# Whole DFT tables and DMA transposes in a fused Fourier and feed-forward kernel

## The chip, the cores and the metric

The kernel runs on one core of one Trainium2 chip. The metric is the device time of one execution, in microseconds; the kernel before takes 851.64 us (median of 3 runs, 851.37 to 852.25).

Names in what follows: PE is TensorE, which does the matmuls (PEld: its weight loads), ACT is ScalarE, DVE is VectorE, POOL is GpSimd; SP is the sync engine, whose queue issues most of the transfers (SPq in the traces). An evacuation is the copy of a matmul's result from PSUM to SBUF, by ACT or DVE.

## The reference

Two layers, one after the other, over 8 batches of 3008 tokens with 256 channels:

```python
X = rfft(x, axis=1)                       # x: (8, 3008, 256)
Yr = Xr @ w_r - Xi @ w_i + b_r
Yi = Xr @ w_i + Xi @ w_r + b_i
Yr, Yi = soft_threshold(Yr, 0.01), soft_threshold(Yi, 0.01)
y = irfft(Yr + 1j * Yi, n=3008, axis=1)   # (24064, 256) tokens for the next layer
h = y @ w_in                              # 256 -> 2048
g = s * maximum(h, 0) ** 2 + b
out = g @ w_out                           # 2048 -> 256, float32
```

The kernel writes 3008 as 94 x 32 and does each transform in two steps as matmuls with tables. The additive b leaves as a bias: b times the sum of w_out over its 2048 rows.

## The kernel before

Batch 0 is transformed first. From then on the feed-forward layer runs in 48 tiles of up to 512 tokens, 16 slots each (a slot is about 1.05 us), and the transform of the next batches is woven into the slots by a plan: the first step (`s1_units`), the second step with mixing and inverse (`s23_units`) and the last step (`s4_units`). The parts that the change and the argument touch:

```python
# x of a batch: four loads of 376 KB with a cast, issued from GpSimd; 4 buffers in all,
# so the loads for batch b+1 wait until the first step of batch b has read its own
def emit_load_x(b, first=None):
    for c in range(N2 // XCH):
        t = xpool.tile([P, XCH * D], F16, name="x16", tag="x16")
        if first is not None:
            gate = nc.gpsimd.tensor_copy(out=t[0:1, 0:1], in_=first)
        ...  # nc.gpsimd.dma_start(out=t[0:N1, ...], in_=xv[...])

# first step: tokens come out on the wrong axis; DRAM turns them
def s1_units(b, more_banks=False):
    ud = dpool.tile([96, N2, D], F16, name="ud", tag="ud")       # DRAM
    def unit(i):                                                 # 16 units a batch
        nc.tensor.matmul(ps[0:96, :], A_t[0:N1, :],              # 512 columns
                         x16[(b, c)][0:N1, j * D : (j + 2) * D], ...)
        evac(u[0:96, j : j + 2, :], ps[0:96, :], 512)
        ...  # u -> ud by DMA, and after the last unit ud -> us, four DMAs

# feed-forward: relu on ACT, square mostly on DVE
nc.scalar.activation(out=rt, in_=ps, func=AF.Relu)
nc.vector.tensor_tensor(out=gt, in0=rt, in1=rt, op=ALU.mult)

# sum of w_out for the bias, on GpSimd, during batch 0
def sum_w_out():
    nc.gpsimd.tensor_tensor(out=acc, in0=w_out_t[:, 0:2], in1=w_out_t[:, 2:4], op=ALU.add)
    for q in range(4, MC, 2):
        nc.gpsimd.tensor_tensor(out=acc, in0=acc, in1=w_out_t[:, q : q + 2], op=ALU.add)
    nc.gpsimd.tensor_tensor(out=w_sum, in0=acc[:, 0], in1=acc[:, 1], op=ALU.add)

# the plan for batches 2 to 7; s0, s1, s2 are the first slots of batches b-2, b-1, b
schedule(s0 + 40, s1 - s0 - 48, s1_units(b))     # first step: spread over most of a batch
schedule(s1 + 2, s2 - s1 - 30, s23_units(b))
schedule(s2 - 14, 12, s4_units(b))
if b + 1 < B:
    plan.setdefault(s1 + 6, []).append(lambda b=b: emit_load_x(b + 1))
```

In batch 0, the block-shaped tables F_t, F_2 and T_t are put together by ACT and DVE from compact ones, and each half of the result e is turned by 32 matmuls with the identity and four evacuations.

## Time and profile before

| | before |
|---|---|
| median of 3 runs (range) | 851.64 us (851.37 to 852.25) |
| profiled run: span, granted TensorE clock | 849.4 us, 0.997 |
| feed-forward tiles 0, 2, 6 and 47 (of 0 to 47) begin at | 49.6, 77.3, 149.3, 823.8 us |

TensorE (PE) is the bound after 58 us. First, when the loads of x are issued. This is the order of time on GpSimd (start us, duration us, engine, line, operation, count, and in brackets the idle time before it and what ended that):

```profile
113.50 0.52 POOL L189 DMA_DIRECT2D x<-in_x_dram  x1 [14.25 <-PE psf L562]
125.97 0.52 POOL L189 DMA_DIRECT2D x<-in_x_dram  x1 [11.95 <-PE psf L562]
138.50 0.52 POOL L189 DMA_DIRECT2D x<-in_x_dram  x1 [12.01 <-PE psf L562]
```

Each load is released by the first step (L562) of the batch before it, and because that step is spread out, so are the loads: one every 12.5 us. In the table of DMA issues (count, size, median us from issue to landing) they land fast:

```profile
x<-in_x_dram POOLq DMA_DIRECT2D x28, 376.0 KB, 5.9
```

Second, GpSimd's sums and DVE's squares, from the order of time on each. The six equal sums take 7.31 us, some 1.2 each, before the squares of the feed-forward tiles set in; those run at 10.31/9 = 1.15 us each:

```profile
40.84 7.31 POOL L331 TENSOR_TENSOR acc<-acc,w_out_t 128x512 f32<-128x512 f32 x6
```

```profile
54.91 10.31 DVE L775 TENSOR_TENSOR gt<-rt 128x1024 f16<-128x1024 f32 x9
```

A stretch of the steady state to compare with (stretch, length, busy us and counts of PE, PEld, DVE, ACT, POOL, then granted clock, DMA share, GB/s). PE is full:

```profile
150.00:158.00 8.00, 8.00 (x67) 6.29 (x66) 5.91 (x9) 5.92 (x9) 0.00 (x0) 1.00 0.47 138
158.00:166.00 8.00, 8.00 (x64) 6.33 (x63) 7.30 (x13) 5.47 (x8) 0.00 (x0) 1.00 0.18 49
```

### The profile page before, as it was taken

The page shows a single profiled execution, that of the slowest core. Times are in us where ns is not written, and L with a number is a line of the kernel's source. Part 1 is how long each engine was busy: PE and PEld are TensorE (multiplying, and loading weights), DVE is VectorE, ACT ScalarE, POOL GpSimd, SP SyncE. Part 2 cuts the span into 40 slices and gives each one's busy share as a digit, 9 for nine tenths or more (in the row PEclk, how much of TensorE's full clock was granted, in tenths as well). Part 3 has the DMA queues.
Part 4 walks back from the last instruction along what each step waited for, and adds up shares of the span by engine and source line. Part 5 has one row for each costly group of instructions (what it writes and reads, how often), then busy time and mean ns, then how long its engine had stood idle before and what let it go on. Part 6 is the DMA issues. An engine that isn't in the chain of part 4 may idle for free.

```text
span 849.4 us, 17085 instructions
## 1 busy us (share of the span) xinstructions
PE 835.0 (98%) x6645; PEld 600.5 (71%) x6645; DVE 697.0 (82%) x1027; ACT 643.2 (76%) x856; POOL 46.6 (5%) x72
## 2 busy tenths in 40 slices
PE   8899999999999999999999999999999999999997
PEld 7757777777677766777677776777667777766765
DVE  6898987888888987888878888888977888776674
ACT  5898887787778787787777887787877787766673
POOL 5321000000000000000000000000000000000000
PEclk9999999999999999999999999999999999999999
DMA  7937457324761367324662247613354223411111
GB/s 165 161 104 162 108 148 185 101 76 100 177 186 54 92 159 184 109 78 103 171 177 65 74 106 199 172 40 92 100 156 118 62 79 98 112 33 38 38 44 50
DMA packets 105458, 95.07 MB, mean 112 GB/s; under 512 B 9510, under 2 KB 97578, under 8 KB 104034
## 3 DMA queue, kind: packets, MB, share of 16 engines
q1 hardware_dynamic: 98930, 79.57, 32.6%
q0 software_dynamic: 6448, 14.42, 10.7%
q8 instruction: 52, 0.85, 0.4%
q14 instruction: 28, 0.23, 0.1%
HBM read 52.54 MB, written 46.66 MB: 117 GB/s over the span
## 4 chain that ended last, share of the span: by engine, by line
PE 88%; DVE 4%; ACT 3%; DMA 2%; issue 1%; POOL 0%; SPq 0%; DVEq 0%; ACTq 0%; POOLq 0%
PE psa L832 36%; PE psh L761 36%; PE psf L627 4%; PE psf L562 2%; PE psf L613 2%; PE psf L598 2%; PE psf L657 2%; PE psf L710 2%; ACT rt L768 1%; DVE gt L775 1%; DMA x<-in_x_dram 1%; DMA out_dram<-ost 1%; PE psh L410 1%; ACT yt L160 0%; ACT vs L160 0%
## 5 line engine op out<-in xcount | busy, mean ns | idle before, releaser
L768 ACT ACTIVATE rt<-psh 128x1024 f32<-128x1024 f32 (+2 forms) x384 | 387.1, 1009 | 119.1 <-PE psh L761 117.7
L775 DVE TENSOR_TENSOR gt<-rt 128x1024 f16<-128x1024 f32 (+2 forms) x321 | 384.0, 1199 | 98.1 <-ACT rt L768 97.4
L832 PE MATMUL psa<-w_out_t,gt 128*128 128x256 f16 (+1 forms) x3024 | 454.3, 272 | 0.1
L832 PEld LDWEIGHTS <-gt 128*128 128x128 f16 (+1 forms) x3024 | 300.9, 101 | 187.2 <-issue 1.7
L761 PE MATMUL psh<-yt,w_in 128*128 128x512 f16 (+1 forms) x1344 | 396.7, 378 | 0.3 <-ACT rt L768 0.3
L761 PEld LDWEIGHTS <-w_in 128*128 128x128 f16 x1536 | 142.9, 98 | 27.4 <-issue 2.1
L842 DVE SCALAR_TENSOR_TENSOR ost<-psa,s_bc,bias_bc 128x512 f32<-128x512 f32 (+2 forms) x97 | 71.0, 732 | 8.3 <-PE psa L832 7.1
L772 ACT ACTIVATE gt<-rt 128x1024 f16<-128x1024 f32 (+2 forms) x63 | 66.2, 1050 | 1.0
L632 DVE TENSOR_TENSOR ring<-psf,s 128x512 f16<-128x512 f32 x84 | 57.5, 684 | 3.7 <-PE psf L627 2.9
L160 ACT CAST v<-psf 128x512 f16<-128x512 f32 x78 | 45.3, 582 | 18.7 <-PE psf L657 18.7
L160 ACT CAST xf<-psf 128x512 f16<-128x512 f32 x82 | 47.9, 585 | 10.9 <-PE psf L598 10.8
L160 ACT CAST u<-psf 96x512 f16<-96x512 f32 x77 | 44.5, 580 | 11.0 <-PE psf L562 10.7
L761 PE MATMUL psh<-tail,w_in 128*128 128x512 f16 (+1 forms) x192 | 52.1, 353 | 0.0
L627 PE MATMUL psf<-W_g,xf 128*128 128x256 f16 x336 | 50.4, 273 | 0.0
L160 ACT CAST yt<-psf 128x480 f16<-128x480 f32 (+2 forms) x75 | 38.1, 520 | 13.6 <-PE psf L710 13.6
L189 POOL DMA_DIRECT2D x<-in_x_dram x36 | 18.9, 530 | 429.3 <-PE psf L562 428.0
L562 PE MATMUL psf<-x,A_t 94*96 94x512 f16 x104 | 39.7, 381 | 1.7 <-ACT yt L160 0.5
L638 DVE TENSOR_TENSOR ring<-ring,high 128x512 f16<-128x512 f16 x84 | 35.5, 423 | 2.3
L639 DVE TENSOR_TENSOR ring<-ring 128x512 f16<-128x512 f16 x84 | 35.5, 422 | 1.9
L637 DVE TENSOR_TENSOR ring<-ring,low 128x512 f16<-128x512 f16 x84 | 35.4, 421 | 1.6
L627 PEld LDWEIGHTS <-xf 128*128 128x128 f16 x336 | 32.9, 98 | 3.8
L710 PE MATMUL psf<-C_t,vs 96*128 96x96 f16 x448 | 33.0, 205 | 0.1
(89 smaller groups left out, 501.9 us busy)
## 6 DMA issues: line engine op xcount, KB each, us to landing
out_dram<-ost SPq DMA_DIRECT2D x152, 128.0 KB
ud<-u SPq DMA_DIRECT2D x28, 384.0 KB
us<-ud SPq DMA_DIRECT2D x28, 384.0 KB
vd<-v SPq DMA_DIRECT2D x42, 256.0 KB
vs<-vd SPq DMA_DIRECT2D x14, 768.0 KB
x<-in_x_dram POOLq DMA_DIRECT2D x28, 376.0 KB, 5.9
ring<-ring SPq DMA_DIRECT2D x280, 32.0 KB
out_dram<-ost SPq DMA_DIRECT2D x16, 120.0 KB
```

What stands on the lines that cost most here:

```text
L160: return None, nc.scalar.copy(out=dst, in_=src)
L562: nc.tensor.matmul(ps[0:96, :], A_t[0:N1, :], x16[(b, c)][0:N1, j * D : (j + 2) * D], start=True, stop=True,)
L627: nc.tensor.matmul(ps[:, r, :], xt[:, 2 - r, dc], W_g[:, dc, r], start=(dc == 0), stop=(dc == DC - 1),)
L632: nc.vector.tensor_tensor(out=t, in0=ps, in1=hold[i // 2][:, i % 2].unsqueeze(1).to_broadcast([P, 2, D]), op=ALU.add,)
L638: nc.vector.tensor_tensor(out=m, in0=m, in1=high, op=ALU.min)
L710: nc.tensor.matmul(ps[:, j * 96 : (j + 1) * 96], vs[(b, h)][:, k, ec * P : (ec + 1) * P], C_t, start=True, stop=True,)
L761: nc.tensor.matmul(o, w_in_t[dc][:, mc * P : (mc + 1) * P], r, start=(dc == 0), stop=(dc == DC - 1),)
L768: nc.scalar.activation(out=rt[:, :, 0:w], in_=ps[:, :, 0:w], func=AF.Relu)
L772: nc.scalar.activation(out=gt[:, :, 0:w], in_=rt[:, :, 0:w], func=AF.Square)
L775: nc.vector.tensor_tensor(out=gt[:, :, 0:w], in0=rt[:, :, 0:w], in1=rt[:, :, 0:w], op=ALU.mult)
L832: nc.tensor.matmul(ps[0:size, h, :], gts[(ti, mc // 2)][:, mc % 2, sub * size : (sub + 1) * size], w_out_t[:, mc, :], start=(mc == 0), sto ...
L842: nc.vector.scalar_tensor_tensor(out=ost[0:size, 0:k], in0=ps[0:size, 0:k], scalar=s_bc[0:size], in1=bias_bc[0:size, 0:k], op0=ALU.mult, o ...
```

## The change

Its intent: less work for PE in the first step of batches 2 to 7 (the data as the weight, 96 columns a matmul), with the turn done by two DMA transposes a batch from SBUF instead of a trip through DRAM; and in batch 0 fewer copies on ACT and DVE (the tables are loaded whole) and one half of e turned by one DMA transpose. Since that transpose stands ahead of the load of w_out, the sums of w_out come later, and the bias is made later. The diff, cut to its core (cuts marked, pool and buffer sizes left out):

```diff
     def emit_load_inverse():
-        nc.sync.dma_start(out=F_c[:, H:]..., in_=F_d[:, H:])
-        t_load = nc.sync.dma_start(out=T_c, in_=T_d)
+        nc.sync.dma_start(out=T_t[:, 0:H], in_=t_d[:, 0:H])        # whole tables
+        nc.sync.dma_start(out=F_t[:, H:], in_=f_d)
+        nc.sync.dma_start(out=F_2[1], in_=f_2_d)
+        t_load = nc.sync.dma_start(out=T_t[:, H:], in_=t_d[:, H:])
 ...
-        nc.gpsimd.dma_start(out=w_out_t, in_=moe_w_out...)         # beside w_in
 ...
-            k = i - U - 2
-            if 0 <= k < 4:
-                turn(0, k)
-            if 0 <= k - 1 < 4:
-                last_dft(0, 8 * (k - 1))
+            if i == U + 1:
+                nc.sync.dma_start(out=vs[0][:, :, 0:P],            # turn_by_dma(0)
+                                  in_=vt[0]..., transpose=True)
+                gate = nc.gpsimd.tensor_copy(out=w_out_t[0:1, 0, 0:1], in_=vs[0][0:1, 0, 0:1])
+                with tc.issue_after(gate.ins):
+                    nc.gpsimd.dma_start(out=w_out_t, in_=moe_w_out...)
 ...
+        def unit_late(i):                                          # first step, b = 2..7
+            for j in range(4):
+                nc.tensor.matmul(
+                    ps[:, j * 96 : j * 96 + 96], x16[(b, c)][0:N1, lo : lo + P],
+                    A_t[0:N1, :], start=True, stop=True,
+                )
+            evac(u[:, dc, :, 4 * g : 4 * g + 4], ps[:, 0:384]..., 384)
+            if g == N2 // 4 - 1:                                   # twice a batch
+                nc.sync.dma_start(
+                    out=us[b][:, :, dc * P : (dc + 1) * P],
+                    in_=u[:, dc].rearrange("p k n -> p (k n)"), transpose=True,
+                )
 ...
-    plan.setdefault(15, []).append(make_bias)
+    plan.setdefault(22, []).append(make_bias)
 ...
-        schedule(s0 + 40, p - 48, s1_units(b))
+        schedule(s1 - 36, 22, s1_units(b))
```

## The prediction

> **What bounds the kernel now.** I read the busy times of each engine first, then the stretches (busy time by window), then the order of time on PE, to get the pace of each shape of matmul, and last the first 58 us on ACT and DVE.
>
> The busy times put PE at 98%, but its ends are modelled, so that alone proves little.
>
> ```profile
> PE 835.0 (98%) x6645; PEld 600.5 (71%) x6645; DVE 697.0 (82%) x1027; ACT 643.2 (76%) x856; POOL 46.6 (5%) x72
> ```
>
> The stretches (busy us of PE, PEld, DVE, ACT, POOL, then granted clock, DMA share, GB/s) cut the run in two:
>
> ```profile
> 0.00:14.60 14.60, 11.60 (x144) 10.73 (x144) 7.71 (x17) 6.08 (x12) 8.13 (x16) 0.88 0.81 165
> 14.60:58.00 43.40, 38.09 (x416) 28.50 (x417) 38.42 (x61) 37.16 (x57) 18.76 (x22) 1.00 0.65 131
> 58.00:150.00 92.00, 91.52 (x717) 65.33 (x715) 80.36 (x125) 73.94 (x103) 4.90 (x12) 1.00 0.63 155
> 150.00:300.00 150.00, 149.87 (x1181) 111.00 (x1180) 128.25 (x204) 117.73 (x160) 3.18 (x5) 1.00 0.42 110
> 450.00:600.00 150.00, 149.95 (x1173) 107.53 (x1172) 128.99 (x202) 117.33 (x158) 3.00 (x5) 1.00 0.39 103
> ```
>
> After 58 us PE is never free. Between 14.6 and 58 us (batch 0's transform and the first tile) PE, DVE and ACT are each busy for 37 to 38.5 of 43.4 us: there the evacuations of PSUM are as much the limit as PE is. Before 14.6 us the load of x sets the pace.
>
> The order of time on PE (start, us, x how many) gives the pace, as the distance from a row to the next one:
>
> ```profile
> 143.61 0.38 PE L710 MATMUL psf<-C_t,vs 96*128 96x96 f16 x5
> 143.82 0.57 PE L761 MATMUL psh<-yt,w_in 128*128 128x480 f16 x2
> ...
> 233.03 0.60 PE L832 MATMUL psa<-w_out_t,gt 128*128 128x256 f16 x4
> 233.47 0.38 PE L562 MATMUL psf<-x,A_t 94*96 94x512 f16 x1
> 233.69 0.60 PE L761 MATMUL psh<-yt,w_in 128*128 128x512 f16 x2
> 234.12 0.60 PE L832 MATMUL psa<-w_out_t,gt 128*128 128x256 f16 x4
> ```
>
> 96 columns take 0.21/5 = 0.042 us, 256 take 0.44/4 = 0.11, the first step's 512 columns 0.22, the other 512 0.43/2 = 0.215. From all start-to-start distances of the trace I took off columns/2.4 + 2.5 ns for each matmul: 15.2 us are left over before 60 us, and only 5.6 us in the other 789 us. So after 60 us the time is the sum of PE's paces, and only what changes that sum counts there.
>
> **What the Trainium skill says.** "TensorE: Matmul & The Clock Gate", Back-to-back issue gap, has N/2.4 + 2.5 ns when warm; the trace agrees at 96, 128, 256 and 512 columns (42, 56, 109, 216 ns medians). The same section gives about 81 ns for a sustained stream of weight load and matmul at N = 128; here that stream runs at 56, so I use the trace. For the DMA transpose, "DMA: Bandwidth & Descriptors", Latency and other measured facts, gives 261 GB/s, 350 to 400 if contiguous; "VectorE: DVE Perf Modes", The three transpose paths, gives 1309 ns for one 128x128 by the DMA crossbar. One transpose here is 24 such blocks (0.79 MB) or 32 (1.05 MB): by the first page an estimate of 3 to 4 us, by the second, if blocks go one by one, 31 and 42 us. The trace of the kernel before holds no DMA transpose and can't decide. "DMA: Bandwidth & Descriptors", Issuing engines are not separate DMA queues, says that all queues share the same 16 engines; the trace agrees: from 20 to 38 us the casting loads of x and the weights alone fill them (DMA share about 1).
>
> **Part 1: the first step of batches 2 to 7.** Removed: 16 matmuls of 512 columns a batch, 16 x 0.22 = 3.52 us of PE. Added: 64 of 96 columns with x as the weight, the shape that batch 0 uses already, 64 x 0.042 = 2.69 us. Gain 0.83 us a batch, 5.0 us for six, all on the path because PE is the bound. Evacuations become 16 of 384 columns (0.48 us on ACT, 0.56 on DVE in batch 0's rows) for 16 of 512 (0.58 and 0.68): off the path. The trip through DRAM (1.57 MB written and read again a batch) becomes two transposes from SBUF. They hurt only if they land late. The second one is issued about 14 slots before its batch's tiles and is needed 2 slots after their start. A slot is (849.4 - 57.8)/752 = 1.05 us, so there are some 17 us for the second and 28 for the first. By order of the SP queue they stand behind the load of vs, ahead of stores only. The next load of x (8 us by its rate here) and the vs load (1.57 MB) fall into the same stretch; together with 2 x 0.79 MB at 200 GB/s this is about 20 us in 30. I expect them hidden.
>
> **Part 2: batch 0.** Removed from ACT and DVE (order of time, ACT and then DVE):
>
> ```profile
> 17.66 0.83 ACT L304 COPY F_t<-F_c 64x768 f16<-64x768 f16 x1
> 19.10 0.83 ACT L304 COPY F_t<-F_c 64x768 f16<-64x768 f16 x1
> 32.70 1.02 ACT L160 CAST vs<-psh 96x1024 f16<-96x1024 f32 x1
> ```
>
> ```profile
> 17.00 1.52 DVE L321 COPY T_t<-T_c 32x768 f16<-32x768 f16 x4
> 21.29 0.45 DVE L311 TENSOR_SCALAR F<-F_c 64x384 f16<-64x384 f16 x1
> 24.11 1.44 DVE L321 COPY T_t<-T_c 32x768 f16<-32x768 f16 x4
> ...
> 37.57 1.21 DVE L164 CAST vs<-psh 96x1024 f16<-96x1024 f32 x1
> ```
>
> That is 1.66 us of F_t copies, 2.96 of T_t copies, 1.06 of second-half F copies (21.29 to 22.35), and four evacuations of the turned first half (1.02 + 1.01 + 1.21 + 1.01 = 4.25): 9.9 us. The two bias copies (1.0 us) move from the first tile to the second, where PE is the bound. 10.9 us over two engines is 5.4 us at most. PE loses 32 turning matmuls, 32 x 0.055 = 1.8 us; its paces in this stretch sum to 36.1 us before (96 x 0.109 + 96 x 0.056 + 4 x 0.216 + 48 x 0.056 + 64 x 0.056 + 64 x 0.042 + 16 x 0.22 + 32 x 0.216) and 34.3 after, of 43.4.
>
> Step by step: up to the last inverse matmuls of the first half (their evacuation ended at 31.45) the copies stand in the alternating chain of g, m and z; I give 2.0 us of the 5.7 to the path. In the six steps after it, evacuations fall from about 12 us (4 turns, 8 last-step, 6 first-step) to 7.5 (12 first-step): half of 4.5 is 2.2. From there to the first matmul into psa of the feed-forward (57.76) PE is nearly full, and both halves' last step now lie there (32 matmuls more, 1.35 us; 6 first-step units less, 1.3): no gain, and some 0.2 lost. Sum: 4.0 us.
>
> Against it: the whole tables load 1.57 MB where 0.59 was loaded. At the 575 KB per 2 us that the SP queue moved from 14 to 16 us, that is 5.5 us from 14 on; the first halves land near 16 to 18, the last near 20, and are used at 20 to 24. The loads of x of batch 1 and w_in start about 0.7 us later. No stall expected.
>
> The load of w_out now waits for the transpose: issued near 29.5, landed at 35 to 40, then GpSimd's queue, 6 us of load (its small packets took 32 to 38 us before) and 9.3 us of sums (39.6 to 49.0 before): bias ready at 53 to 57. It is needed 6 slots into the second tile, near 58.
>
> **Sum.** 851.6 - 5.0 - 4.0 = 842.6 us.
>
> **The rivals.** (a) Slow transposes. At 31 us each, one after another, the second would land 62 us after the issue of the first, for which there are 28: over 30 us of PE standing a batch, and over 1000 us in all. At 15 us nothing is seen in the steady part, but in batch 0 w_out and the bias come 5 us late and PE waits for both: 846 to 848. For it: the 1309 ns of the page. Against it: two pages give rates ten times higher, and the new schedule leaves 17 us, which is no room for 31. (b) The evacuations of the first part are hidden anyway, as PE there is 88% busy: then only 5.0 + 1.8 come, 845. Against it: 15 us of left-over distance before 60 us. (c) Density: 16 first-step units in 22 slots instead of some 48 put evacuations on ACT and DVE where the second and third steps still run (8 slots); both are near 85% busy on average. A wait of 0.5 us a batch would make 845. (d) Everything comes: 5.4 us in batch 0 and some of the 5.6 left over: 839 to 840. A win over 2% (under 834.6) would need all 15 us of left-over distance: shut out, for 5.7 of them lie in the load of x.
>
> **Range and chances.** 838.5 to 848 holds (b), (c), (d) and the mild form of (a). Within 2%: 0.93; slower by over 2% (it takes 26 us of new waits against the 9 gained, over 4 us a batch, so only slow transposes do it): 0.05; faster: 0.02.
>
> **What would show it.** Right: the matmuls of the first step of batches 2 to 7 at 42 ns, PE still full after 58 us, the first second-layer matmul at about 53.8 instead of 57.76, the transposes landing within 10 us. Wrong: idle time of PE before the second step of a batch released by a transpose, a wait for w_out or for the bias in the second tile, or stores held in the SP queue behind a transpose until the three ost buffers run out.

## The result, and the profile after

The changed kernel takes 894.4 us (median of 4 runs, 891.49 to 907.48) against 851.71 for the kernel before in the same rounds: 1.0476 times as long, interval 1.043 to 1.0523. It is slower by nearly 5%, and the results are right. Ratios here are the mean time of one kernel's fast runs over that of the other's of the same rounds, so not quite the ratio of the medians that are quoted. The profiled run was slow (907.5 us), so the lines below are from a second set of runs of the same kernel, whose profiled run was a fast one (run e1_again, span 901.9 us). The slow runs have 905.40 and 907.48 us at a clock of 0.973, the fast run of the profile 903.66 at 0.971.

The page's busy times and the clock in 40 slices:

```profile
PE 846.1 (94%) x6901; PEld 611.6 (68%) x6901; DVE 694.2 (77%) x1016; ACT 637.0 (71%) x850; POOL 55.2 (6%) x73
...
PEclk9899999899998999899997999979999999999999
```

PE was 98% busy and is 94% now; DVE and ACT are no busier. So the time went into waits, and the clock dips at intervals. The waits (engine, line, what was waited for, us in total, times, longest) name two that the kernel before didn't have:

```profile
PE psf L630 <- DMA us<-u: 34.9, 9, 6.1
...
DVE ost L872 <- DMA out_dram<-ost: 23.3, 5, 6.2
```

L630 is the second step, which reads the transposed `us`. The starts of the tiles show where the time goes. The table gives the difference from the kernel before, for the start of a tile (us):

| tile | 1 | 2 | 6 | 7 | 12 | 13 | 17 | 18 | 23 | 24 | 29 | 30 | 47 |
|---|---|---|---|---|---|---|---|---|---|---|---|---|---|
| after less before | 0.0 | +6.3 | +5.4 | +14.1 | +14.6 | +23.2 | +21.8 | +28.9 | +29.5 | +41.0 | +41.5 | +52.8 | +52.5 |

There is one step of 6.3 us between tiles 1 and 2, and then five of 8.7, 8.6, 7.1, 11.5 and 11.3 us: 47.2 in sum, one where each of the batches 2 to 6 begins its second step. The rest is a gain of 1.0. Batch 7 has no step. These are two separate losses.

**The five steps.** First GpSimd, in the order of time, as above:

```profile
130.87 0.52 POOL L200 DMA_DIRECT2D x<-in_x_dram  x1 [55.91 <-PE psf L574]
...
138.87 0.51 POOL L200 DMA_DIRECT2D x<-in_x_dram  x1 [2.44 <-PE psf L574]
```

The loads of x are still released by the first step, now L574. But that step is packed into 22 slots just ahead of its transposes, so all four loads come within 8 us, at the very time of the transposes. The sync queue (start, how long the queue was held):

```profile
129.71 24.91 SPq L583 DMA_TRANSPOSE us<-u  x1
...
156.21 5.52 SPq L583 DMA_TRANSPOSE us<-u  x1
161.83 3.17 SPq L817 DMA_DIRECT2D out_dram<-ost  x5
```

The first transpose holds the queue for 24.9 us; the second can't be issued before 156.21, and stores stand behind both. PE meets the result in its order of time:

```profile
155.96 0.60 PE L862 MATMUL psa<-w_out_t,gt 128*120 128x256 f16 x4
160.98 0.29 PE L630 MATMUL psf<-F_t,us 128*128 128x128 f16 x1 [4.43 <-DMA us<-u]
163.88 0.50 PE L630 MATMUL psf<-F_t,us 128*128 128x128 f16 x3 [2.62 <-DMA us<-u]
164.18 1.06 PE L791 MATMUL psh<-yt,w_in 128*128 128x512 f16 x2
```

Two waits, 7 us together, and then the pair of 512-column matmuls takes 1.06 us where 0.60 is usual. The stretches that stood at full PE before read now:

```profile
150.00:158.00 8.00, 6.55 (x53) 4.60 (x51) 3.80 (x4) 4.64 (x7) 0.00 (x0) 1.00 1.24 82
158.00:166.00 8.00, 2.40 (x12) 1.68 (x13) 3.24 (x4) 0.58 (x1) 0.00 (x0) 0.61 0.82 157
```

In the second one PE is busy for 2.40 of 8 us, and the granted clock is 0.61. In the trace's record of the clock it falls to one half at 159.7 us, 3.1 us after PE fell idle, and stays there for 6.8 us. Each of the five steps has one such stretch, of 6.8 or 10.2 us, that begins 2 to 4.5 us after PE first stops; e6, e11 and e12 below, which have no such waits, have none between 60 and 840 us. So each wait costs more than itself: 34.9 us of waits for `us`, 47.2 us of steps. This fits with the spread of this kernel's fast runs, from 889.0 to 903.7 us, while those of the kernel before beside them agree within a fifth of a per cent.

The load of x suffers as well; its median time to landing goes from 5.9 to

```profile
x<-in_x_dram POOLq DMA_DIRECT2D x28, 376.0 KB, 17.8
```

Counting the DMA packets of the trace by queue shows what the two transfers do to one another. The load of x moves in packets of mostly 4096 bytes, a transpose in packets of 256:

```
after (e1_again)     load of x          sync queue
us                packets    KB       packets    KB
136 to 138             24    98           396   185
138 to 140             24    86            35     9
140 to 142             80   266           108    28
142 to 144             73   258            77    20
144 to 146             86   303            95    24
146 to 148             76   258           244    62
148 to 150             33   102           360    92
150 to 152             21    74           129    33
152 to 154             17    57           146    37
154 to 156              9    29           503   129
156 to 158              5     8          1040   275
```

Until 137 us the sync queue still moves the load of vs ahead of the transpose (packets of 8192 bytes), so some 6 of the 24.9 us are not the transpose's own; the same transpose behind the same load, but without x, holds the queue for 8.32 us (e2 below). From 140 to 146 us the counts of packets are nearly equal, and the bytes are ten to one. The Trainium skill has this rule: each DMA engine goes round-robin between the queues that have work for it, packet by packet ("DMA: Bandwidth & Descriptors", Queues, rings and completion order). If the profile's packets are those of the page, the counts of these 6 us agree with it. So does an estimate from the durations on record there: 322 ns for a packet of x and 31 for one of the transpose (medians), so 16 engines that take turns would move 16/0.353 = 45 of each in a us, 11.6 KB of the transpose. It moved 10 to 14 KB in a us, where alone it moves 290 (shown below). Before and after these 6 us turns are not the whole of it. From 138 to 140 us both queues move little. From 150 to 154 us only a few packets of x are left and the transpose still creeps, with the DMA share above 1: the median of its packets is then on record for 322 ns, as long as one of x, instead of 31 (18 when alone). Why, no run shows.

**The 6 us by tile 2.** GpSimd's sums of w_out now stand here, and DVE's squares beside them:

```profile
56.19 12.50 POOL L332 TENSOR_TENSOR acc<-acc,w_out_t 128x512 f32<-128x512 f32 x6
```

```profile
52.74 20.06 DVE L805 TENSOR_TENSOR gt<-rt 128x1024 f16<-128x1024 f32 x11 [0.32 <-ACT rt L798]
```

The six sums take 12.50 us for 7.31; the records of single instructions give 2.02 us a sum and 2.17 a square (1.15 and 1.22 alone), each starting every 2.10 us: one square, one sum, in turn. The Trainium skill says why ("SBUF — State Buffer", SBUF: two separate sides, and Who interferes with whom): VectorE and GpSimd share one pair of SBUF ports, a VectorE instruction with two inputs in SBUF contends with a GpSimd instruction that reads SBUF, and the later one waits for the whole instruction. The square has two such inputs (rt twice), and the trace agrees, nearly: wholly one after the other, by the starts alone (1.14 and 1.23 us apart before the change), a pair would take 2.37 us, so they overlap a little. That it is the two inputs that matter, no run here tests. Seven squares that start every 2.10 us instead of 1.14 are 6.7 us, about the 6.3 of the table.

### The profile page after: what moved, and what is told of

Its sections match the earlier page's. It is cut to its first block, busy times and chain, and to the rows that moved or that the text cites. A ratio compares the mean times of both kernels' runs of the same rounds, so it can differ in the third digit from the quotient of the medians.

```text
span 905.7 us, 17513 instructions
## 1 busy us (share of the span) xinstructions
PE 844.8 (93%) x6901; PEld 611.2 (67%) x6901; DVE 694.5 (77%) x1016; ACT 637.3 (70%) x850; POOL 54.8 (6%) x73
## 4 chain that ended last, share of the span: by engine, by line
PE 81%; DVE 8%; DMA 6%; ACT 2%; issue 1%; SPq 0%; POOL 0%; DVEq 0%; ACTq 0%; POOLq 0%
PE psa L862 33%; PE psh L791 32%; DMA us<-u 4%; PE psf L659 4%; DVE gt L805 3%; PE psf L630 2%; PE psf L740 2%; PE psf L645 2%; PE psf L574 2%; PE psf L689 2%; DMA x<-in_x_dram 1%; DVE ring L664 1%; PE psh L418 1%; DVE ring L681 1%; DVE ost L872 1%
## 5 line engine op out<-in xcount | busy, mean ns | idle before, releaser
L791 PE MATMUL psh<-yt,w_in 128*128 128x512 f16 (+1 forms) x1344 | 403.0, 382 | 3.2 <-ACT rt L798 3.1
L791 PEld LDWEIGHTS <-w_in 128*128 128x128 f16 x1536 | 138.4, 99 | 18.4 <-issue 4.8
L802 ACT ACTIVATE gt<-rt 128x1024 f16<-128x1024 f32 (+2 forms) x68 | 71.4, 1050 | 1.0
L630 PE MATMUL psf<-F_t,us 128*128 128x128 f16 x336 | 35.4, 229 | 37.6 <-DMA us<-u 37.6
L630 PEld LDWEIGHTS <-us 128*128 128x128 f16 x336 | 26.9, 102 | 41.8 <-DMA us<-u 39.7
L636 DVE TENSOR_TENSOR xf<-xf 128x256 f16<-128x256 f16 x84 | 24.0, 287 | 33.6 <-ACT xf L171 33.2
L200 POOL DMA_DIRECT2D x<-in_x_dram x36 | 18.8, 528 | 449.3 <-PE psf L574 448.2
L171 ACT CAST yt<-psf 128x480 f16<-128x480 f32 (+2 forms) x69 | 34.9, 525 | 11.3 <-PE psf L740 11.0
L171 ACT CAST u<-psf 128x384 f16<-128x384 f32 (+1 forms) x71 | 34.4, 487 | 11.8 <-PE psf L574 11.7
```

The costliest lines, as they stand in the source:

```text
L171: return None, nc.scalar.copy(out=dst, in_=src)
L630: nc.tensor.matmul(ps[:, :, dc, j, :], us[b][:, 2 * i + j, dc * P : (dc + 1) * P], F_t[:, 2 * i + j, :], start=True, stop=True,)
L791: nc.tensor.matmul(o, w_in_t[dc][:, mc * P : (mc + 1) * P], r, start=(dc == 0), stop=(dc == DC - 1),)
L802: nc.scalar.activation(out=gt[:, :, 0:w], in_=rt[:, :, 0:w], func=AF.Square)
```

## The experiments

All were run against the kernel before on the same chip: e1 to e4 on one, e5 to e8 on a second, e9 to e12 on a third. All results were right. The diffs are against the changed kernel.

**e1_again**: no edit, the changed kernel once more.

> The changed kernel again, for a profile in the fast state: its profiled run was a slow one (907 us). Theory A (the load of the next x, released by the first step, holds back the two DMA transposes, and PE waits for them before the second step of batches 2 to 6): 887 to 897 us; five idle stretches of PE before the second step, 4 to 10 us each, none for batch 7, which has no x behind it; some 6 us lost in the second tile. Rival B (the transposes are slow by themselves): the same time, but then batch 7 should wait too, and it did not in the first profile.

900.2 us (891.28 to 903.66), ratio 1.055 (1.049 to 1.0611). The loss is there again. Its profile is the one above.

**e2_x_gated**: x of batch b+1 is loaded only when the second transpose of batch b has landed. Nothing else is touched, and the transposes stay where they are.

```diff
-            plan.setdefault(s1 + 6, []).append(lambda b=b: emit_load_x(b + 1))
+            plan.setdefault(s1 + 6, []).append(
+                lambda b=b: emit_load_x(b + 1, us[b][0:1, 0, D - 1 : D])
+            )
```

> Only change: the load of x of batch b+1 (b from 2) starts after the second transpose of batch b has landed. Theory A: the five stretches go, each transpose lands in 4 to 9 us, the run falls by about 40 us, to 846 to 856. Rival B (transposes slow by themselves, or held by the load of vs or by the SP queue): the waits stay, over 880. Rival C (x then comes too late): a new wait before the first step of batches 3 to 7.

856.76 us (854.93 to 857.72), ratio 1.0054 (1.0039 to 1.0069). All five steps are gone: the difference from the kernel before stays between +5.1 and +7.7 us from tile 2 to the end, and no wait for `us` or for a store is left among those of PE and DVE. The sync queue (order of time):

```profile
131.26 8.32 SPq L583 DMA_TRANSPOSE us<-u  x1
...
140.93 5.74 SPq L583 DMA_TRANSPOSE us<-u  x1
```

So the load of x beside the transposes makes the five steps, some 43 us of the loss, and not the transposes as such.

**e3_x_dummy_last**: the opposite. Batch 7 has no load of x beside its transposes and no step; here it gets one that nobody reads.

```diff
-        if b + 1 < B:
-            plan.setdefault(s1 + 6, []).append(lambda b=b: emit_load_x(b + 1))
+        plan.setdefault(s1 + 6, []).append(lambda b=b: emit_load_x(min(b + 1, B - 1)))
```

> Only change: batch 7 also gets a load of x behind its first step (x of batch 7 again, into the same buffers, never used; results stay right). Theory A: a sixth wait before the second step, 6 to 10 us long, at about 700 us of the profile, where there was none. Rival B (batch 7 is free of waits because its transposes meet fewer stores or a lighter schedule): still none.

One run, state unknown, 913.62 us. The time of one run proves little, the place does: between tiles 35 and 36 there is now a sixth step of 10.6 us (51.9 to 62.5 behind the kernel before; e1_again stays at 52.6). Order of time on the sync queue and on PE; in e1_again the queue was held here for 8.21 us:

```profile
673.33 22.51 SPq L583 DMA_TRANSPOSE us<-u  x1
```

```profile
709.36 0.50 PE L630 MATMUL psf<-F_t,us 128*128 128x128 f16 x3 [7.55 <-DMA us<-u]
```

**e4_sum_on_pe**: the sums of w_out leave GpSimd; the bias is made by 16 accumulating matmuls of ones with w_out. The load of x is left as in the changed kernel.

```diff
-        nc.tensor.matmul(ps[:, 0:D], ones, w_sum, start=True, stop=True)
+        for mc in range(MC):
+            nc.tensor.matmul(
+                ps[:, 0:D], ones, w_out_t[:, mc, :], start=(mc == 0), stop=(mc == MC - 1)
+            )
 ...
-                    sum_w_out()
```

> Only change: the column sums of w_out for the bias, eight additions on GpSimd, become 16 accumulating matmuls of 256 columns with ones (1.75 us of PE) where the one matmul stood. Theory D (the late w_out puts GpSimd's additions beside the squares of the first tiles, and DVE and GpSimd slow each other: 1.9 to 2.1 us for a square instead of 1.22): the squares of the first tile go back to 1.22 us, tile 2 starts 4 to 6 us earlier, the run gets 3 to 5 us faster than the changed kernel of the same state. Rival: the squares are slow for another reason (DMA into SBUF): no change, or 1.7 us slower.

892.05 us (890.1 to 894.81), ratio 1.0481 (1.0458 to 1.0505). Tile 2 begins at 77.3 us, as before the change, instead of 83.5, and the squares run at 7.01/6 = 1.17 us again (order of time on DVE):

```profile
56.48 7.01 DVE L807 TENSOR_TENSOR gt<-rt 128x1024 f16<-128x1024 f32 x6 [0.59 <-ACT rt L800]
```

The steps stay, though unevenly: 1.6, 13.6, 0.5, 16.5 and 7.5 us in this profile. So the second loss is that of the squares and sums side by side. The ratios put it at 1.055 - 1.0481, about 6 us, within the spread of these kernels.

**e5_gated_sum_pe**: the edits of e2 and e4 together.

> Both edits that helped alone, together: x of the next batch after the transposes, and the bias sums on PE. If the two losses are separate, they add: 856.8 - 6.2 = 850.6 us (849 to 852), the same as the kernel before within 0.3%. If one hides behind the other, it stays at 853 or above.

850.9 us (849.27 to 851.26), ratio 0.9988 (0.9972 to 1.0005). Against e2's 1.0054 that is 0.66% less, or 5.6 us: the two losses are separate and add up. But with both gone, only some 1 us of the gain is seen, and the interval takes in none at all.

**e6_gated_sum_pe_spaced**: e5, with the late first step nine slots later, in 18 slots instead of 22. In e2 and e4 PE waits 0.2 to 1.1 us a batch, 4.3 us in all six, where the first units of the late first step meet the last of the inverse step; an example from e2's order of time on PE:

```profile
223.46 0.33 PE L574 MATMUL psf<-A_t,x 94*128 94x96 f16 x4 [1.08 <-DVE u L175]
```

```diff
-        schedule(s1 - 36, 22, s1_units(b))
+        schedule(s1 - 27, 18, s1_units(b))
```

> As e5, but the first step of batches 2 to 7 runs in slots -27 to -9 before its tiles instead of -36 to -14, behind the last inverse step of the batch before. Theory E (density: where the first step meets the end of the inverse step, it waits some 1.25 us a batch for a PSUM bank, which eats its gain): these waits, 5 us in all in the profile of e2, go, and the run is 3 to 5 us faster than e5. Rival: the second transpose now has 11 slots instead of 16 and lands late (waits before the second step come back), or the last step beside it waits instead: no gain.

846.82 us (846.28 to 847.56), ratio 0.9946 (0.9931 to 0.9961); 4.1 us under e5, on the same chip. The waits of PE before the first step add up to 4.3 us in e2 and e5 (not the 1.25 a batch of the expectation) and to 0.5 here, so they are nearly the whole gain. This profile also shows a transpose alone, with no load of x near:

```profile
138.32 3.60 SPq L585 DMA_TRANSPOSE us<-u  x1
```

The trace's packets give 1133 packets and 290 KB in the us from 133 to 134, for the other transpose of this batch. That lies between the two figures of the page that the prediction took, 261 GB/s and 350 to 400.

**e7_gated_w_out_early**: e2, with the load of w_out back beside w_in, ahead of the transpose of batch 0, so that GpSimd sums early again.

```diff
+        nc.gpsimd.dma_start(out=w_out_t, in_=moe_w_out.rearrange("(mc p) d -> p mc d", p=P))
 ...
-                gate = nc.gpsimd.tensor_copy(out=w_out_t[0:1, 0, 0:1], in_=vs[0][0:1, 0, 0:1])
-                with tc.issue_after(gate.ins):
-                    nc.gpsimd.dma_start(out=w_out_t, ...)
```

> As e2 (x gated), with the load of w_out back beside w_in, no longer behind the transpose of batch 0, and the sums on GpSimd again. Theory D: GpSimd's sums end before the first tile, the squares take 1.22 us, and the run is 6 to 8 us faster than e2 (849 to 851). Rival (the reason the edit put w_out behind): the transpose shares its time with w_out's 512-byte packets, lands at 45 us or later instead of 40, and PE waits for it before the last step of batch 0: a gain under 4 us.

856.01 us (854.92 to 856.14), ratio 1.005 (1.0035 to 1.0065): no better than e2. The sums are back at 1153 ns each, but now the transpose of batch 0 shares the DMA engines with w_out (packets of 512 bytes; from 34 to 44 us the counts per 2 us are 285 to 272, 455 to 455, 229 to 225, 468 to 496, 393 to 419, again one to one). PE waits for it (order of time on the sync queue and on PE):

```profile
29.96 15.63 SPq L494 DMA_TRANSPOSE vs<-vt  x1
```

```profile
47.83 0.50 PE L506 MATMUL psf<-C_t,vs 96*128 96x96 f16 x4 [5.61 <-DMA vs<-vt]
```

One loss is traded for the other. The gate ahead of w_out had a reason.

**e8_x_small_packets**: the changed kernel, with x of batches 3 to 7 loaded in pieces of 128 columns, so that its packets are small and equal turns give the transposes a larger share of the bytes.

```diff
+            if b > 2:
+                for i in range(2):       # every second block of 128 columns
+                    nc.gpsimd.dma_start(out=t...(h=2, k=P)[:, i], in_=src...(h=2, k=P)[:, i])
```

> The changed kernel with x of batches 3 to 7 loaded in 256-byte pieces (two strided transfers a tile in place of one in 4096-byte packets), still not gated. Theory A1 (the engines alternate packet by packet, so a 256-byte transpose packet waits for a 4096-byte one of x): the transposes get an even share, the first lands within about 12 us and the waits of PE before the second step fall from 5 to 10 us to under 4, though x takes longer. Theory A2 (any load from the other queue slows a transpose, whatever its packets): the waits stay or grow, since x now takes longer.

One run, state unknown, 908.24 us: no gain. The share of the transposes rose as the rule of equal turns says: from 152 to 157 us some 330 packets a us on either side, the transpose at 85 KB/us instead of 10 to 14. The hold times don't show this. The first transpose held the queue for 8.8 us instead of 24.9, but the packets of x came only from 140 us on, when that hold was over; the second, beside x, held it for 13.7 instead of 5.5. PE's wait for the transposes fell from 34.9 to 18.8 us. But the edit did more than intended: beside the packets of 256 bytes the trace has 211,568 of 4 bytes on the queue of x, where e1_again has 728. The load of x itself became long, and other small transfers now wait beside it (waits):

```profile
PE psf L639 <- DMA us<-u: 18.8, 4, 7.0
DVE ring L673 <- DMA ring<-ring: 18.1, 6, 4.9
```

The counts bear the equal turns out; because of the 4-byte packets the time of this run says nothing of small packets as a remedy. What helped in the other runs was to keep the two apart in time.

**e9_late_only**: the batch 0 of the kernel before, and the late first step with its transposes as in the change.

```diff
 # against the kernel before: its batch 0 is kept
-        schedule(s0 + 40, p - 48, s1_units(b))
+        schedule(s1 - 36, 22, s1_units(b))       # made of unit_late
```

> The kernel before with only part 1 of the change (first step of batches 2 to 7 through DMA transposes, x not gated); batch 0 as before. Theory A: part 1 alone brings the five waits: 851.7 + about 43 of waits (e1 less e2), so 886 to 900 us, and the squares of the first tile stay at 1.22 us. If the waits need batch 0's part too, it stays under 870.

902.28 us (896.27 to 909.19), ratio 1.0569 (1.0528 to 1.061). Part 1 alone brings the steps; tile 2 begins only 1.4 us late.

**e10_batch0_only**: the new batch 0, with the first step of batches 2 to 7 through DRAM as before.

```diff
-        schedule(s1 - 36, 22, s1_units(b))
+        schedule(s0 + 40, p - 48, s1_units(b, late=False))
```

> The changed kernel with the first step of batches 2 to 7 taken back to the matmuls of 512 columns, the trip through DRAM and the old schedule; only part 2 (batch 0) stays. Theory D: batch 0 is 3.6 us faster up to the first second-layer matmul, and loses 7 to 8 to the squares beside GpSimd's sums: 853 to 857 us, no wait before the second step. My prediction's part 2 as written would give 847.7.

858.28 us (856.92 to 858.91), ratio 1.0074 (1.0059 to 1.0089), 1 us above what was expected. Tile 1 begins 2.0 us early and tile 2 6.6 us late; from there the difference grows only to 7.6. DVE beside the sums (order of time), and then PE, which here waits for the bias as well (1.2 us in e2, not at all in e1_again):

```profile
51.18 19.82 DVE L805 TENSOR_TENSOR gt<-rt 128x1024 f16<-128x1024 f32 x11 [0.32 <-ACT rt L798]
```

```profile
69.97 0.27 PE L337 MATMUL psa<-w_sum,ones 128*128 128x256 f16 x1 [2.85 <-POOL w_sum L333]
```

**e11_best_pe_turn**: the whole tables and the late first step, gated and spaced as in e6; the first half of e in batch 0 turned on PE as in the kernel before; w_out beside w_in and the sums on GpSimd.

```diff
-            if i == U + 1:
-                turn_by_dma(0)
-                ...                                     # gate and load of w_out
+            k = i - U - 2
+            if 0 <= k < 4:
+                turn(0, k)
+            if 0 <= k - 1 < 4:
+                last_dft(0, 8 * (k - 1))
 # with the edits of e2 and the spacing of e6
```

> x gated and the first step in slots -27 to -9 as in e6, whole tables as in the changed kernel, but batch 0's first half turned on PE again as before, with the load of w_out beside w_in and the sums on GpSimd. Against e6 (846.8): PE gains 16 matmuls of the sums (1.75 us) and loses 32 turning ones (1.8 us), ACT and DVE get four evacuations back (half of 4.25 us, not all on the path): 846 to 849. If the DMA transpose of batch 0 is worth its place, e6 stays ahead by 1 us or more.

845.24 us (844.7 to 845.6), ratio 0.9922 (0.9908 to 0.9937): the fastest of all, 0.8% ahead of the kernel before. PE is full again (busy times):

```profile
PE 830.7 (98%) x6933; PEld 605.4 (72%) x6933; DVE 688.6 (82%) x1023; ACT 638.9 (76%) x847; POOL 51.8 (6%) x92
```

**e12_late_gated_spaced**: e9 with the gate of e2 and the spacing of e6, so part 1 by itself without its faults.

```diff
 # against e9
-        schedule(s1 - 36, 22, s1_units(b))
+        schedule(s1 - 27, 18, s1_units(b))
-            plan.setdefault(s1 + 6, []).append(lambda b=b: emit_load_x(b + 1))
+            plan.setdefault(s1 + 6, []).append(
+                lambda b=b: emit_load_x(b + 1, us[b][0:1, 0, D - 1 : D])
+            )
```

> The kernel before with part 1 mended (x gated behind the transposes, first step in slots -27 to -9), batch 0 as before. Theory: with the waits gone only the pace is left, 6 x (16 x 0.216 - 64 x 0.0425) = 4.4 us, and the 1.8 us that matmuls stood waiting for the first step's banks before: 846 to 848. If part 1 has another cost that e6 hides, it stays above 849.

847.5 us (847.39 to 848.11), ratio 0.9951 (0.9936 to 0.9966). So part 1 is worth about 4.2 us, and the whole tables of batch 0, with the new order of the steps that goes with them (the first step of batch 1 earlier, the bias later), the 2.3 us between this and e11.

| run | what differs from the changed kernel | median us | ratio to before |
|---|---|---|---|
| after / e1_again | nothing | 894.4 / 900.2 | 1.0476 / 1.055 |
| e2 | load of x gated | 856.76 | 1.0054 |
| e3 (one run, state unknown) | a load of x for batch 7 too | 913.62 | none |
| e4 | sums on PE | 892.05 | 1.0481 |
| e5 | gated, sums on PE | 850.9 | 0.9988 |
| e6 | gated, sums on PE, first step later (spaced) | 846.82 | 0.9946 |
| e7 | gated, w_out early | 856.01 | 1.005 |
| e8 (one run, state unknown) | x of batches 3 to 7 in small packets | 908.24 | none |
| e9 | batch 0 of before | 902.28 | 1.0569 |
| e10 | first step of before | 858.28 | 1.0074 |
| e11 | gated, spaced, turned on PE, w_out early | 845.24 | 0.9922 |
| e12 | gated, spaced, batch 0 of before | 847.5 | 0.9951 |

## Why the prediction was wrong

It put the time at 842.6 us, within 2% of before, with 0.93. The result is 5% slower. By its own steps:

- **"I expect them hidden"** is the step that failed. It added up the bytes of the stretch (two transposes, the load of x, the load of vs) and divided by 200 GB/s: "about 20 us in 30" (its own terms, 8 us of x and 3.15 MB at 200 GB/s, make 24). That takes the DMA engines for a pipe that shares its bytes. Where the two overlapped most (140 to 146 us) the packets were shared one to one, and a transpose with packets of 256 bytes got about a tenth of the bytes of a load whose packets are mostly 4096. The first transpose held the queue for 25 us instead of the estimated 3 to 4 (8.3 in e2, behind the load of vs alone), the second stood behind it in the queue, and the load of x, released by the very first step that ends in the transposes, met both in five of six batches. The prediction had listed the load of x in the stretch, and looked only at its bytes. e2 took the load away (43 us back), e3 added one (a sixth step), and in e8, with small packets of x, the counts stayed equal and the transpose's bytes rose to 85 KB/us.
- **Rival (a), slow transposes**, named the right symptom with the wrong reason. It asked whether the transpose is slow by itself, by two figures of the skill, and took the fast one. The fast one is right (290 KB/us alone). What made it slow was its neighbour. Of the three signs that the prediction listed as "wrong", two came in the changed kernel: PE idle before the second step, released by a transpose, and stores held behind one until the buffers ran out (23.3 us of DVE's waits). The third, a wait for the bias in the second tile, came in e10 (2.85 us) and e2 (1.2). What it didn't foresee is the half clock after each long wait, part of the 12 us between the waits and the steps.
- **"Bias ready at 53 to 57"** failed by 13 us, and its consequence was mis-seen. Its terms: the transpose landed at 42.6 instead of 35 to 40, the load of w_out took 10 us instead of 6, and the sums 16 us (53.95 to 70.3) instead of 9.3. The prediction counted on a wait of PE for the bias at most. The main cost lay elsewhere: the moved sums fell beside the squares and slowed them from 1.22 to 2.17 us. e4 shows it, 6 us.
- **Rival (c), density**, came nearly as sized: 0.5 us a batch were estimated, 0.7 measured (4.3 us over six batches in e2), and e6 took 4.1 us off. But it was the meeting with the inverse step and not the density: e6 packs the same units closer, into 18 slots, behind that step.
- **The pace of the first step** was right: its 384 matmuls lie 42 ns apart in the median. The term of 5.0 us was slightly high: freed of its faults, part 1 gives 4.2 (e12).
- **Part 2's 4.0 us** were half right. The first second-layer matmul came at 54.5 us (e1_again; 53.8 predicted, 57.76 before). But e11, without the DMA transpose of batch 0, has it at 54.4: the gain came with the whole tables and the new order around them, not with the transpose that was to spare PE 32 matmuls. And at the end 2.3 us of it remain (e11 against e12). Of the 9.0 us that the prediction counted on, e11 gets 6.2.

What stays open: why a transpose still creeps when only a few packets of the other queue are left (150 to 154 us above), and so how much of the 43 us comes from the equal turns and how much from this. That the load of x is the cause is shown by e2 and e3; no experiment here took apart how it does it.

## What to carry to other kernels

When two transfers overlap, count packets as well as bytes: here the one with packets of 256 bytes got a tenth of the bytes of the one with 4096. In this kernel the DMA transposes needed a stretch of their own, and what is released by the same step (the next load, through a buffer coming free) had to be gated until they had landed. When an operation is moved, ask what it will stand beside: sums on GpSimd that cost nothing at 40 us cost 6 us at 56, where they met squares on VectorE that read two operands from SBUF. And with PE full, look at what a moved step will meet before counting its gain; the same units nine slots later were worth 4 us.

## What the Trainium skill lacked or had wrong

- "DMA: Bandwidth & Descriptors", Queues, rings and completion order, has the round-robin by packet, but says nowhere near it what that does to a DMA transpose: 256-byte packets against 4096-byte ones, 10 to 14 KB/us instead of 290, the sync queue held for 24.9 us instead of 8.3 (e2; 3.6 with nothing beside it, e6).
- The same page, Rules for kernel authors, says "A transpose next to ordinary DMAs needs nothing". The row is about corrupted results, and all results here were right; for the time it doesn't hold: a load of x beside the transposes cost 43 us (e1_again against e2).
- The same page, Latency and other measured facts, gives 261 GB/s for a transpose, 350 to 400 if contiguous, and no figure beside other traffic: 290 KB/us alone in e6 (one us of a transpose), 10 to 14 beside a load of x.
- "VectorE: DVE Perf Modes", The three transpose paths, gives 1309 ns for one 128x128 by DMA; 24 such blocks in one transpose hold the queue for 3.6 us here (e6), so the figure can't be multiplied by the number of blocks.
- "TensorE: Matmul & The Clock Gate", Back-to-back issue gap, gives about 81 ns for a stream of weight load and matmul at N = 128; 56 ns here.
- "SBUF — State Buffer", Who interferes with whom, has the contention right, but no figure for this pair: square and sum every 2.10 us, 2.17 us for 1.22 and 2.02 for 1.15. Its rule that the later one waits for the whole instruction would make that 2.37 us at least.
